# Pooled attention and two expert layers on one core: second layer's weights converted in pairs of blocks with their last addition on GpSimd, and the leading tiles' attention work put into other steps

## The chip, the cores and the metric

The kernel runs on one core of a Trainium2 chip. The metric is device time in microseconds (us), from the first to the last instruction of the program. Three executions of the kernel before took 1326.18, 1326.63 and 1329.12 us; their median, 1326.63 us, is its time.

## The reference

Everything is float32. With 12288 queries of 128 channels (`q`, multiplied by 8 after it is drawn), a map `kv` of 384 x 32 positions, and `d_ff = 2048`:

```
kv_pool = mean of kv over 4 x 4 windows            # 96 * 8 = 768 keys
k = v = kv_pool @ w_sr                             # 768 x 128
a = exp(s - max(s)),  s = q @ k.T / sqrt(128)
x = (a / (sum(a) + 1e-9)) @ v
h = x @ w_in;   g = h * sigmoid(1.702 * h);        x = g @ w_out     # layer 1
h = x @ w_in2;  g = h * clip(h + 3, 0, 6) / 6;     out = g @ w_out2  # layer 2
```

## The kernel before

**Two-part numbers.** A product of float32 numbers is made of three products of float32r numbers on TensorE. Each operand is split into a high part (`..h`, or `hi`, rounded by ScalarE, helper `act_hi`) and the rest (`..l`, or `lo`, mostly a subtraction on VectorE, `dve_lo`; for `q` on GpSimd, `pool_lo`). So one float32 product is low*high, high*high and high*low.

**The weights' conversion.** The four weight matrices reach the chip as float64 bit patterns, two 32-bit words for each weight, in 16 blocks of 512 columns (`ws`, 128 x 512 x 2 words; eight blocks for each layer). VectorE makes float32 of the words. `w_bits` has four instructions (L180, L183, L186, L190), `w_hi` one on ScalarE, and `w_lo` four on VectorE (L202, L205, a subtraction on L133, the last addition on L212). `w_lo` also asks for a later block's load. Blocks 0 to 4 are converted in the opening (`W_EARLY`, and the piece `W` of `FIRST`), blocks 5 to 15 in the steps of `W_STEPS`: `w_bits` at step s, `w_hi` and `w_lo` at s+1.

**The opening.** Loads of `kv` (12 of 512 KB) and of the first blocks stand in SP's queue; pooling and the product with `w_sr` are one chain of matmuls (L541), which yields `k` and `v`. Then the list `FIRST` gives the order in which TensorE makes scores of tiles 0 to 3 (`S`), transpositions (`T`) and products with `v` (`A`). A tile is 512 queries, 24 tiles in all.

**The steps.** The rest is a loop over 384 units (layer, tile, j), one unit a step: tiles 0 to 3 in layer 1 (steps 0 to 31), the same in layer 2 (steps 32 to 63), then two tiles after another, 16 steps for each layer. In step s TensorE does the first product of unit s (`unit_mm`, 6 matmuls into one of two PSUM buffers `h`) and the second product of unit s-3 (`unit_out`, 6 matmuls into `acc`). In between ScalarE applies GELU and splits off `gh`, VectorE makes `gl` (L133); in layer 2 ScalarE makes `r` (L446) and VectorE `g` (L450). The two PSUM buffers of `acc` are also those of the attention's products with `v`.

**Attention beside the steps.** Tables of step numbers put the attention of later tiles into the steps. Tiles 2 and 3 are transposed on TensorE (`T_STEPS_0`, L288, into the single PSUM buffer `st`, emptied by ScalarE to `eTh` and VectorE to `eTl`). From tile 4 on VectorE transposes 32 x 32 blocks (`V_STEPS`, L307), 16 DMAs move them (`D_STEPS`), and three steps split the result (`H_STEPS`: `eTh` on ScalarE, `eTl` on VectorE). The product with `v` follows in two halves (`AV_STEPS`, `av_mm`, L341). Scores (`S_STEPS`, L241) also use `st`; VectorE takes the maximum (L248) and ScalarE the exponential. GpSimd multiplies by the reciprocal sums (L280) and makes the low part of `q` (L136). The tables with `_0` hold for the first 64 steps. Within a step `ORDER` sets the order on ScalarE and VectorE.

The engines run their instructions in the order in which the program lists them (the scheduler is off).

Of the kernel before, what the change touches and what calls it, by code (L numbers as in the profile page):

```python
# [76 lines left out]
def tile_pooled_attention__moe_gelu__moe_hardswish(  # L77
# [39 lines left out]
    wi = {}  # L117
    wo = {}
    for m in (1, 2):
        wi[m] = [const.tile([P, DFF], F32R, name=f"wi{m}_{s}") for s in "hl"]  # L120
        wo[m] = [const.tile([P, DFF], F32R, name=f"wo{m}_{s}") for s in "hl"]
# [40 lines left out]
    w_todo = []  # L162
    w_ready = []
    w_half = []
    w_places = list(W_PLACES)

    def w_load(tag):
        w, src, cs = w_todo.pop(0)
        s = work.tile([P, WL, 2], U32, tag=tag, name="ws", bufs={"g": 3, "r": 2, "ws": 1}[tag])
        nc.sync.dma_start(out=s, in_=src[:, cs, :])  # L170
        w_ready.append((w, s, cs))

    def w_bits():


        w, ws, cs = w_ready.pop(0)
        upper = ws[:, :, 1]
        a = work.tile([P, WL], U32, tag="o", name="wa")
        b = work.tile([P, WL], U32, tag="wb", name="wb")
        nc.vector.tensor_scalar(  # L180
            out=a, in0=upper, scalar1=0x7FFFFFFF, scalar2=None, op0=ALU.bitwise_and
        )
        nc.vector.tensor_scalar(  # L183
            out=f(a), in0=f(a), scalar1=UPPER_MIN, scalar2=UPPER_MAX, op0=ALU.max, op1=ALU.min
        )
        nc.vector.tensor_scalar(  # L186
            out=b, in0=a, scalar1=3, scalar2=0x3FFFFFFF,
            op0=ALU.logical_shift_left, op1=ALU.bitwise_and,
        )
        nc.vector.scalar_tensor_tensor(  # L190
            out=a, in0=upper, scalar=0xC0000000, in1=b, op0=ALU.bitwise_and, op1=ALU.bitwise_or
        )
        w_half.append((w, ws, cs, a, b))
# [229 lines left out]
    for s in W_STEPS:  # L423
        at(s, "w_bits", w_bits)
        at(s + 1, "w_hi", w_hi)
        at(s + 1, "w_lo", w_lo)
# [63 lines left out]
    with tc.manual_schedule():  # L490
        make_identity(nc, ident)
        for m, src_i, src_o in ((1, w_in1, w_out1), (2, w_in2, w_out2)):
            blocks = [slice(o, o + WL) for o in range(0, DFF, WL)]
# [35 lines left out]
        for g_ in range(n_g):  # L529
            pk = big(*slots[g_])[:, 0, :kg]  # L530
            for w_ in range(n_w):
# [3 lines left out]
                if i in W_EARLY:  # L535
                    w_bits()
                    w_hi()
                    if i != W_EARLY[-1]:
                        w_lo()
# [114 lines left out]
```

## Time and profile before

| | |
|---|---|
| median of three executions | 1326.63 us (1326.18 to 1329.12) |
| span of the profiled execution | 1327.1 us |
| TensorE (PE) busy | 1299.5 us, 98% |
| VectorE (DVE) busy | 1038.1 us, 78% |
| ScalarE (ACT) busy | 1011.3 us, 76% |
| GpSimd (POOL) busy | 156.9 us, 12% |
| mean granted TensorE clock | 0.996 of full speed |

The profiled execution's span is the only time the page gives of it; no further time lies around it, and it is 0.5 us over the median of the three. Busy shares are averages over stages with different limits. A matmul is pipelined, so its busy time runs on while the next has begun; what counts on TensorE are the gaps, in which nothing ran, and the clock that was granted.

### The profile page before, as it was taken

How to read it: one execution, taken by the hardware profiler on the slowest of the kernel's cores; microseconds unless marked ns; L12 is line 12 of the kernel's file. 1: busy time of each engine (PE TensorE's matmuls, PEld its weight loads, DVE VectorE, ACT ScalarE, POOL GpSimd, SP SyncE). 2: the span in 40 equal slices, each digit the busy share in tenths (PEclk: the TensorE clock that was granted, in tenths of full speed). 3: DMA queues.
4: the chain of work that ended last, by engine and by line, in shares of the span. 5: the costliest groups of instructions: out<-in, count | busy, mean ns of one | idle time of the engine just before them, and what ended most of it. 6: DMA issues, size and time to landing. Idle time of an engine off the chain costs nothing.

```text
span 1327.1 us, 16044 instructions
## 1 busy us (share of the span) xinstructions
PE 1299.5 (98%) x5814; PEld 1077.7 (81%) x5814; DVE 1038.1 (78%) x1069; ACT 1011.3 (76%) x1191; POOL 156.9 (12%) x126
## 2 busy tenths in 40 slices
PE   8989999899999999999999999999999999999998
PEld 6778888777888888888888888788788888878887
DVE  6888899877688688688688688778768868858567
ACT  2777777668778778778878877787877877877876
POOL 0410003111011011011011002001101101100000
PEclk9999999999999999999999999999999999999999
DMA  8111102202202202201300400310220220210000
GB/s 319 41 48 48 33 16 64 64 8 61 51 16 57 56 16 56 56 17 30 82 9 11 108 9 9 86 26 17 62 50 17 56 56 9 56 48 8 9 1 17
DMA packets 26528, 59.84 MB, mean 45 GB/s; under 512 B 6352, under 2 KB 6480, under 8 KB 26448
## 3 DMA queue, kind: packets, MB, share of 16 engines
q1 hardware_dynamic: 26304, 58.75, 15.7%
q8 instruction: 46, 0.75, 0.2%
q14 instruction: 34, 0.28, 0.1%
q10 hardware_dynamic: 144, 0.07, 0.0%
HBM read 21.04 MB, written 6.29 MB: 21 GB/s over the span
## 4 chain that ended last, share of the span: by engine, by line
PE 84%; DVE 7%; ACT 3%; SPq 2%; issue 2%; DMA 2%; DVEq 0%; ACTq 0%
PE acc L473 12%; PE acc L474 12%; PE acc L475 12%; PE h L438 11%; PE h L437 11%; PE h L436 11%; PE acc L341 7%; PE st L241 6%; DVE gl L133 2%; SPq L317 2%; DVE eTl L133 1%; DMA kvs<-kvT 1%; DVE nm L248 1%; DMA q_f<-qT 1%; DVE g L450 1%
## 5 line engine op out<-in xcount | busy, mean ns | idle before, releaser
L133 DVE TENSOR_TENSOR gl<-g,gh 128x1024 fp32r<-128x1024 f32 x384 | 475.8, 1242 | 166.5 <-ACT gh L130 166.4
L130 ACT ACTIVATE gh<-g 128x1024 fp32r<-128x1024 f32 x384 | 405.3, 1058 | 23.7 <-PE acc L474 20.4
L446 ACT ACTIVATE r<-h 128x1024 f32<-128x1024 f32 x192 | 196.9, 1026 | 144.5 <-PE h L438 144.5
L473 PE MATMUL acc<-gh,wo_l 128*128 128x512 f32 x768 | 300.0, 391 | 0.5
L450 DVE SCALAR_TENSOR_TENSOR g<-r,h 128x1024 f32<-128x1024 f32 x192 | 234.1, 1219 | 84.0 <-ACT r L446 82.2
L475 PE MATMUL acc<-gl,wo_h 128*128 128x512 f32 x768 | 299.3, 390 | 0.4 <-DVE gl L133 0.4
L474 PE MATMUL acc<-gh,wo_h 128*128 128x512 f32 x768 | 299.3, 390 | 0.0
L442 ACT ACTIVATE g<-h 128x1024 f32<-128x1024 f32 x192 | 196.2, 1022 | 56.2 <-PE h L438 56.0
L473 PEld LDWEIGHTS acc<-gh,wo_l 128*128 128x128 f32 x768 | 144.3, 188 | 34.7 <-DVE x1l L133 4.3
L475 PEld LDWEIGHTS acc<-gl,wo_h 128*128 128x128 f32 x768 | 144.2, 188 | 31.1 <-DVE gl L133 0.8
L474 PEld LDWEIGHTS acc<-gh,wo_h 128*128 128x128 f32 x768 | 144.3, 188 | 30.7
L280 POOL TENSOR_SCALAR e<-e,rec 128x768 f32<-128x768 f32 x96 | 120.0, 1269 | 280.3 <-issue 201.5
L436 PE MATMUL h<-x1h,wi_l 128*128 128x512 f32 x384 | 150.8, 393 | 0.0
L438 PE MATMUL h<-x1l,wi_h 128*128 128x512 f32 x384 | 150.0, 391 | 0.0
L437 PE MATMUL h<-x1h,wi_h 128*128 128x512 f32 x384 | 149.9, 390 | 0.0
L436 PE MATMUL h<-x2h,wi_l 128*128 128x512 f32 x368 | 143.2, 389 | 1.2 <-DVE g L450 1.2
L438 PE MATMUL h<-x2l,wi_h 128*128 128x512 f32 x368 | 144.3, 392 | 0.0
L437 PE MATMUL h<-x2h,wi_h 128*128 128x512 f32 x368 | 144.0, 391 | 0.0
L136 POOL TENSOR_TENSOR q_l<-q_f,q_h 128x512 fp32r<-128x512 f32 x24 | 36.3, 1511 | 705.6 <-ACT q_h L130 705.6
L263 ACT ACTIVATE e<-st,nm 128x768 f32<-128x768 f32 x86 | 77.1, 896 | 13.1 <-DVE nm L248 13.0
L438 PEld LDWEIGHTS h<-x1l,wi_h 128*128 128x128 f32 x384 | 72.4, 188 | 15.3
L436 PEld LDWEIGHTS h<-x1h,wi_l 128*128 128x128 f32 x384 | 72.4, 188 | 15.0
(90 smaller groups left out, 1423.2 us busy)
## 6 DMA issues: line engine op xcount, KB each, us to landing
eTl<-e SPq DMA_DIRECT2D x320, 96.0 KB, 2.1
kvs<-kvT SPq DMA_DIRECT2D x12, 512.0 KB, 9.6
q_f<-qT SPq DMA_DIRECT2D x24, 256.0 KB, 2.6
outT<-o SPq DMA_DIRECT2D x24, 256.0 KB, 2.0
ws<-w_in SPq DMA_DIRECT2D x8, 512.0 KB, 4.6
ws<-w_out SPq DMA_DIRECT2D x8, 512.0 KB, 4.0
wsr_sb<-w_sr ACTq DMA_DIRECT2D x1, 64.0 KB, 4.7
```

Source lines behind the costliest of these rows:

```text
L130: nc.scalar.activation(hi, x, AF.Copy)
L133: nc.vector.tensor_tensor(out=lo, in0=x, in1=f(hi), op=ALU.subtract)
L280: nc.gpsimd.tensor_scalar(out=e, in0=e, scalar1=rec[:, r:r + 1], scalar2=1.0, op0=ALU.mult, op1=ALU.mult)
L436: nc.tensor.matmul(hp[:, c, :], wi[m][1][:, ch], xh, start=True, stop=False)
L437: nc.tensor.matmul(hp[:, c, :], wi[m][0][:, ch], xh, start=False, stop=False)
L438: nc.tensor.matmul(hp[:, c, :], wi[m][0][:, ch], xl, start=False, stop=True)
L442: nc.scalar.activation(g, h_t.pop(u), AF.Gelu_apprx_sigmoid)
L446: nc.scalar.activation(r, h_t[u], AF.Relu, bias=3.0)
L450: nc.vector.scalar_tensor_tensor(out=g, in0=r_t.pop(u), scalar=6.0, in1=h_t.pop(u), op0=ALU.min, op1=ALU.mult)
L473: nc.tensor.matmul(acc, wo[m][1][:, ch], gh[:, c, :], start=first, stop=False)
L474: nc.tensor.matmul(acc, wo[m][0][:, ch], gh[:, c, :], start=False, stop=False)
L475: nc.tensor.matmul(acc, wo[m][0][:, ch], gl[:, c, :], start=False, stop=last)
```

## The change

The conversion is cut into five parts: `a` and `b` (the four instructions of `w_bits`), `h` (the high part on ScalarE), `c` and `d` (the four of `w_lo`). The eight blocks of layer 1 are converted one at a time as before, those of layer 2 two at a time: each instruction then has 128 x 1024 elements. In these pairs the last addition goes to GpSimd. Raw words and the tiles `g` and `r` share one tile `slots` of five places; all high and low weights lie in `w_hl`; `w_a` and `w_b` have one buffer each, and the output tile `o` takes that of `w_a`. Block 5's parts `a`, `b`, `c` come at the end of `FIRST`, and the loads of blocks 5 to 7 are asked for one conversion later than before (block 5's stood between the last two pieces of `kv`). The step tables of tiles 2 to 5 change.

```diff
-T_STEPS_0 = {2: (4, 6, 8, 10), 3: (14, 16, 18, 20)}
-V_STEPS_0 = {4: (40, 41, 42, 43), 5: (48, 49, 50, 51)}
-D_STEPS_0 = {4: 44, 5: 52}
-H_STEPS_0 = {4: (47, 48, 49), 5: (55, 56, 57)}
-AV_STEPS_0 = {1: (1, 2), 2: (11, 12), 3: (21, 22), 4: (50, 51), 5: (58, 59)}
+T_STEPS_0 = {2: (7, 9, 11, 13), 3: (15, 17, 19, 21)}
+V_STEPS_0 = {4: (40, 41, 42, 43), 5: (50, 51, 52, 53)}
+D_STEPS_0 = {4: 44, 5: 54}
+H_STEPS_0 = {4: (48, 49, 50), 5: (58, 59, 60)}
+AV_STEPS_0 = {1: (1, 2), 2: (14, 14), 3: (22, 22), 4: (52, 53), 5: (61, 62)}
...
-    "S00 Q1 S01 S10 S02 S03 S11 T00 T01 T02 Q2 v T03 S12 S13 S20 A0 W Q3 T10 T11 T12 T13 S21 S22 "
-    "S23 S30 S31 S32 S33"
+    "S00 Q1 S01 S10 S02 S03 S11 T00 T01 T02 Q2 v T03 S12 S13 S20 A0 Wcd Q3 T10 T11 T12 T13 S21 S22 "
+    "S23 S30 S31 S32 S33 Wabc"
...
-W_LOADS = {0: "g", 2: "g", 4: "g", 6: "r", 8: "r", 10: "ws"}
-W_EARLY = (1, 3, 5, 7, 9)
-W_PLACES = "- - - r r ws r r ws r r - r r - -".split()
-W_STEPS = (0, 2, 5, 9, 12, 15, 18, 21, 24, 27, 29)
+W_LOADS = 0, 2, 4, 6, 8
+W_EARLY = {1: "abhcd", 3: "abhcd", 5: "abhcd", 7: "abhcd", 9: "abh"}
+W_SLOTS = 0, 1, 2, 3, 4, 3, 4, 3, 3
+W_NEXT = 0, 0, 0, 1, 1, 1, 0, 1, 1, 1, 1, 0
+W_STEPS = (
+    (0, "hdab"), (2, "hcd"), (3, "ab"), (5, "hcd"),
+    (8, "a"), (10, "b"), (12, "hc"), (14, "d"), (16, "a"), (18, "b"), (20, "hc"), (21, "d"),
+    (22, "a"), (23, "b"), (25, "hc"), (26, "d"), (27, "a"), (28, "b"), (30, "hc"), (31, "d"),
+)
...
+    w_hl = [const.tile([P, len(w_blocks), WL], F32R, name=f"w_{s}") for s in "hl"]
+    slots = const.tile([P, 5, 2 * TT], F32, name="slots")
...
+    def w_group(n):
+        k = len(w_blocks) // 2
+        if n < k:
+            return range(n, n + 1), W_SLOTS[n]
+        return range(2 * n - k, 2 * n - k + 2), W_SLOTS[-1]
...
+        if kind == "d":
+            dve_lo(w_a, w_a, hi)
+            add = nc.vector if k == 1 else nc.gpsimd
+            add.tensor_tensor(out=lo, in0=w_a, in1=w_b, op=ALU.add)
...
-        g_t[u] = g = work.tile([P, 2, TT], F32, tag="g", name="g", bufs=3)
+        g_t[u] = g = slot(u % 3)
...
-        r_t[u] = r = work.tile([P, 2, TT], F32, tag="r", name="r")
+        r_t[u] = r = slot(3 + u % 2)
...
-            o = work.tile([P, TT], F32, tag="o", name="o")
+            o = work.tile([P, TT], F32, tag="w_a", name="o", bufs=1)
```

What moves in the program is told below by rows of the instruction order, where a number at the end tells how often the row follows itself. First VectorE's rows from the last maximum of the opening on, in the kernel before (`wa`, `wb` are the conversion's tiles, `gl` is that of units 0 and 1):

```order
L248 TENSOR_REDUCE nm<-st 128x1
L276 TENSOR_SCALAR rec<-sums 128x4
L277 RECIPROCAL rec<-rec 128x4
L133 TENSOR_TENSOR gl<-g,gh 128x1024
L180 TENSOR_SCALAR wa<-ws 128x512
L183 TENSOR_SCALAR wa<-wa 128x512
L186 TENSOR_SCALAR wb<-wa 128x512
L190 SCALAR_TENSOR_TENSOR wa<-ws,wb 128x512
L133 TENSOR_TENSOR gl<-g,gh 128x1024
L202 TENSOR_SCALAR wb<-wa 128x512
```

And VectorE's rows from the same maximum on in the changed kernel:

```order
L283 TENSOR_REDUCE nm<-st 128x1
L218 TENSOR_SCALAR w_a<-slots 128x512
L221 TENSOR_SCALAR w_a<-w_a 128x512
L225 TENSOR_SCALAR w_b<-w_a 128x512
L229 SCALAR_TENSOR_TENSOR w_a<-slots,w_b 128x512
L236 TENSOR_SCALAR w_b<-w_a 128x512
L239 SCALAR_TENSOR_TENSOR w_b<-slots,w_b 128x512
L311 TENSOR_SCALAR rec<-sums 128x4
L312 RECIPROCAL rec<-rec 128x4
L152 TENSOR_TENSOR gl<-slots,gh 128x1024
L152 TENSOR_TENSOR w_a<-w_a,w_h 128x512
L247 TENSOR_TENSOR w_l<-w_a,w_b 128x512
```

Six of block 5's eight instructions now stand ahead of tile 3's reciprocals and of the first `gl`; its last two, and then block 6's first four, stand between the first and the second `gl`.

GpSimd's rows around the end of layer 1 in the kernel before (`q_l` is the low part of a tile's queries, `e` are the exponentials of a tile):

```order
L136 TENSOR_TENSOR q_l<-q_f,q_h 128x512
L280 TENSOR_SCALAR e<-e,rec 128x768 x8
L136 TENSOR_TENSOR q_l<-q_f,q_h 128x512 x2
L280 TENSOR_SCALAR e<-e,rec 128x24x32 x4
L136 TENSOR_TENSOR q_l<-q_f,q_h 128x512
```

And GpSimd's rows there in the changed kernel:

```order
L155 TENSOR_TENSOR q_l<-q_f,q_h 128x512
L315 TENSOR_SCALAR e<-e,rec 128x768 x8
L247 TENSOR_TENSOR w_l<-w_a,w_b 128x1024 x3
L155 TENSOR_TENSOR q_l<-q_f,q_h 128x512
L247 TENSOR_TENSOR w_l<-w_a,w_b 128x1024
L155 TENSOR_TENSOR q_l<-q_f,q_h 128x512
L315 TENSOR_SCALAR e<-e,rec 128x24x32 x4
```

Four additions of 128 x 1024 have come in, three of them ahead of tile 4's `q_l` and one behind it.

TensorE's rows from the end of step 50's second product on, in the kernel before (`acc<-eT` is tile 4's product with `v`, `st<-k` are scores):

```order
L475 MATMUL acc<-gl,wo_h 128x512
L341 MATMUL acc<-eTh,v_l 128x512 x3
L341 MATMUL acc<-eTh,v_h 128x512 x3
L341 MATMUL acc<-eTl,v_h 128x512 x3
L241 MATMUL st<-k_h,q_h 128x384 x2
L241 MATMUL st<-k_l,q_h 128x384 x2
L241 MATMUL st<-k_h,q_l 128x384 x2
```

TensorE's rows from the same place on in the changed kernel:

```order
L507 MATMUL acc<-gl,w_h 128x512
L276 MATMUL st<-k_h,q_h 128x384 x2
L276 MATMUL st<-k_l,q_h 128x384 x2
L276 MATMUL st<-k_h,q_l 128x384 x2
L468 MATMUL h<-x_1265,w_l 128x512
L469 MATMUL h<-x_1265,w_h 128x512
```

The product with `v` has left step 50; the scores follow the second product at once, and the next step's first product follows them. The nine matmuls stand two steps later.

## Rows read from the trace of the kernel before

**Rows 1.** From the page: TensorE's busy time, and the chain by engine.

```profile
PE 1299.5 (98%) x5814; PEld 1077.7 (81%) x5814; DVE 1038.1 (78%) x1069; ACT 1011.3 (76%) x1191; POOL 156.9 (12%) x126
PE 84%; DVE 7%; ACT 3%; SPq 2%; issue 2%; DMA 2%; DVEq 0%; ACTq 0%
```

**Rows 2.** Stretches: length, each engine's busy time (instructions), granted clock, DMA share, GB/s.

```profile
26.00:28.00 2.00, 1.96 (x10) 1.41 (x9) 1.90 (x7) 0.38 (x1) 0.00 (x0) 1.00 1.04 412
60.00:90.00 30.00, 25.88 (x115) 21.20 (x114) 24.06 (x37) 22.96 (x29) 8.38 (x8) 0.94 0.12 36
90.00:180.00 90.00, 88.14 (x406) 72.58 (x405) 78.92 (x109) 68.78 (x79) 1.41 (x1) 1.00 0.13 39
500.00:600.00 100.00, 99.86 (x448) 83.08 (x447) 77.09 (x75) 79.97 (x94) 13.26 (x10) 1.00 0.16 43
221.04:293.88 72.84, 67.10 (x289) 55.40 (x289) 61.77 (x60) 48.22 (x62) 14.14 (x10) 0.95 0.19 49
```

**Rows 3.** Timeline of TensorE: start, length, instruction, idle before it and what ended that.

```profile
83.46 1.15 PE L288 MATMUL st<-ident,e 128*128 128x128 f32 x6 [4.00 <-DVE eTl L133]
104.37 0.50 PE L341 MATMUL acc<-eTh,v_l 128*128 128x512 f32 x1 [0.68 <-DVE x2l L133]
177.81 0.50 PE L436 MATMUL h<-x2h,wi_l 128*128 128x512 f32 x1 [1.18 <-DVE g L450]
236.37 0.97 PE L341 MATMUL acc<-eTh,v_l 128*128 128x512 f32 x3 [3.14 <-ACT eTh L130]
271.17 1.31 PE L341 MATMUL acc<-eTh,v_l 128*128 128x512 f32 x3 [2.33 <-ACT eTh L130]
322.53 0.73 PE L341 MATMUL acc<-eTh,v_l 128*128 128x512 f32 x2 [1.29 <-ACT eTh L130]
```

**Rows 4.** Timeline of VectorE at the end of the opening and in step 0.

```profile
62.50 0.96 DVE L248 TENSOR_REDUCE nm<-st 128x1 f32<-128x768 f32 x1 [0.38 <-PE st L241]
64.59 0.44 DVE L276 TENSOR_SCALAR rec<-sums 128x4 f32<-128x4 f32 x1 [1.13 <-ACT e L263]
67.95 1.23 DVE L133 TENSOR_TENSOR gl<-g,gh 128x1024 fp32r<-128x1024 f32 x1 [2.71 <-ACT gh L130]
69.55 0.94 DVE L183 TENSOR_SCALAR wa<-wa 128x512 f32<-128x512 f32 x1
71.59 1.22 DVE L133 TENSOR_TENSOR gl<-g,gh 128x1024 fp32r<-128x1024 f32 x1
```

**Rows 5.** Groups of instructions by form: count, busy time, mean ns of one, idle before.

```profile
L133 DVE TENSOR_TENSOR gl<-g,gh 128x1024 fp32r<-128x1024 f32 x384 | 475.8, 1242 | 166.5 <-ACT gh L130 166.4
L133 DVE TENSOR_TENSOR eTl<-st,eTh 128x768 fp32r<-128x768 f32 x10 | 9.5, 950 | 0.1
L183 DVE TENSOR_SCALAR wa<-wa 128x512 f32<-128x512 f32 x16 | 7.4, 460 | 0.5
L212 DVE TENSOR_TENSOR wi_l<-wa,wb 128x512 fp32r<-128x512 f32 x8 | 5.5, 692 | 0.3
L307 DVE STREAM_TRANSPOSE e<-e 128x768 f32<-128x768 f32 x80 | 76.4, 963 | 0.0
L136 POOL TENSOR_TENSOR q_l<-q_f,q_h 128x512 fp32r<-128x512 f32 x24 | 36.3, 1511 | 705.6 <-ACT q_h L130 705.6
```

**Rows 6.** Timeline of GpSimd and VectorE where the two run at once.

```profile
166.92 1.41 POOL L136 TENSOR_TENSOR q_l<-q_f,q_h 128x512 fp32r<-128x512 f32 x1 [96.71 <-ACT q_h L130]
167.08 2.33 DVE L133 TENSOR_TENSOR gl<-g,gh 128x1024 fp32r<-128x1024 f32 x1
226.74 2.78 POOL L280 TENSOR_SCALAR e<-e,rec 128x768 f32<-128x768 f32 x2 [4.95 <-DVE rec L277]
226.87 1.87 DVE L133 TENSOR_TENSOR eTl<-eTl,eTh 128x1024 fp32r<-128x1024 f32 x1 [0.23 <-issue]
```

**Rows 7.** Timeline of TensorE's weight loads at the last `kv` piece.

```profile
27.55 0.19 PEld L541 LDWEIGHTS st<-kvs,wsr_sb 128*128 128x128 f32 x1 [0.44 <-DMA kvs<-kvT]
```

More of the change, by code (lines that the diff above doesn't have):

```diff
@@ L116, in tile_pooled_attention__moe_gelu__moe_hardswish, with chunk, slot @@
     v_l = const.tile([P, KC, C], F32R, name="v_l")
[L117 to L121, printed above, removed]
+    w_blocks, w_at = [], {}
+    for m, src_i, src_o in ((1, w_in1, w_out1), (2, w_in2, w_out2)):
+        blocks = range(DFF // WL)
+        for side, k in sorted(
+            [("i", k) for k in blocks] + [("o", k) for k in blocks],
+            key=lambda x: (max(x[1] * 2 + 3 * (x[0] == "o"), 0), x[0]),
+        ):
+            w_at[side, m, k] = len(w_blocks)
+            w_blocks.append((src_i if side == "i" else src_o, slice(k * WL, (k + 1) * WL)))
+    w_hl = [const.tile([P, len(w_blocks), WL], F32R, name=f"w_{s}") for s in "hl"]
+    slots = const.tile([P, 5, 2 * TT], F32, name="slots")
+    def chunk(side, m, n):
+        k, c = divmod(n, WL // P)
+        return (x[:, w_at[side, m, k], c * P:(c + 1) * P] for x in w_hl)
+    def slot(n):
+        return slots[:, n].rearrange("p (c k) -> p c k", k=TT)
     def f(ap):
@@ L159, in split_q @@
         load_q(t + 1)
[L162 to L193, printed above, removed]
@@ L349, in split_acc @@
     def split_acc(acc, tag, place=None):
-        if place == "ws":
-            both = work.tile([P, 2, TT], F32R, tag="ws", name=tag, bufs=1)
-            hi, lo = both[:, 0, :], both[:, 1, :]
-        else:
-            hi, lo = (
-                work.tile([P, TT], F32R, tag=place or tag + s, name=tag + s) for s in "hl"
-            )
+        if place is not None:
+            both = work.tile([P, 2, TT], F32R, tag=place, name=tag, bufs=1)
+            hi, lo = both[:, 0], both[:, 1]
+        else:
+            hi, lo = (work.tile([P, TT], F32R, tag=tag + s, name=tag + s) for s in "hl")
         act_hi(hi, acc)
@@ L422, in tile_pooled_attention__moe_gelu__moe_hardswish @@
             at(step, "table", exp_table)
[L423 to L426, printed above, removed]
+    for step, kinds in W_STEPS:
+        for kind in kinds:
+            at(step, "w_hi" if kind == "h" else "w", w_step, kind)
     h_t, r_t, g_t, gs_t, acc_t = {}, {}, {}, {}, {}
@@ L535, in tile_pooled_attention__moe_gelu__moe_hardswish @@
                 if i in W_EARLY:
[L536 to L539, printed above, removed]
+                    for kind in W_EARLY[i]:
+                        w_step(kind)
                 for w in range(kw // kg):
@@ L575, in piece @@
             elif kind == "W":
-                w_lo()
+                for step in name[1:]:
+                    w_step(step)
             else:
```

117 lines of the change are left out of this document (74 added, 43 removed).

## The prediction

> **What bounds the kernel now.** I read the page first: TensorE is busy in 98% of the span and has 84% of the chain [rows 1], so only a TensorE gap or a slow clock can be won. The table of stretches, next, shows where there is one: from 500 to 600 us TensorE stands still for 0.14 of 100 us, from 60 to 90 us for 4.1 of 30 at a mean clock of 0.94, and from 221 to 294 us for 5.7 of 72.8 at 0.95 [rows 2]. The order of instructions from step 64 on is the same in both kernels, so the change can only act ahead of that, some 294 us into the span. The timeline of TensorE names each gap there and what ended it [rows 3]: 4.00 us at 83 us (a transposition of tile 2 waits for `st`, which VectorE empties late), 0.68 at 104 (PSUM `acc` held by VectorE's `x2l`), 1.18 at 178 (`h` held by VectorE's `g`), and 3.14 and 2.33 at 236 and 271 us, where the product with `v` waits for `eTh`. All come from a VectorE that is late. In the opening TensorE runs through scores and pooling with small waits of which the change touches one [rows 7].
>
> **The opening.** Block 5's load no longer stands between the last two pieces of `kv`. The DMA engines are full there (share 1.04, 412 GB/s [rows 2]), so 512 KB less ahead of the last piece lets it land 512 KB / 412 GB/s = 1.3 us earlier; TensorE waited 0.44 us for it [rows 7], and no more can be won. I take 0.4, from 0 to 0.4.
>
> **Block 5's six instructions, steps 0 to 9.** By [rows 5] one block costs VectorE four single-input instructions of 0.46 us and four two-input ones of 0.69: 4.6 us. Parts `a`, `b` and `c` are four of 0.46 and two of 0.69, 3.2 us. They go where VectorE is idle: between the last maximum and the first `gl` it stands still for 1.13 + 2.71 = 3.8 us [rows 4]. Tile 2's two early transpositions leave steps 4 and 6 too, with 2 x 0.95 us of VectorE [rows 5], so by step 6 VectorE has 5.1 us less to do than before, more than the 4.00 us that TensorE waited. That wait goes, and with it the slow clock that followed: 0.06 x 30 = 1.8 us [rows 2]. Full gain 5.8.
>
> It isn't free, though. Tile 3's reciprocals now stand behind the six, so GpSimd's four scalings for tile 3 start some 2.5 us later and run beside step 0. What that does is seen in [rows 6]: a subtraction of `eTl` that began with a scaling took 1.87 us in place of 1.2, and two scalings took 2.78 us with the subtraction in between; a `gl` behind a `q_l` took 2.33 us. The two engines take turns, an instruction at a time, when VectorE reads two tensors of SBUF; in [rows 4] the single-input L183 took 0.94 in place of 0.43. A scaling alone is (2.78 - 1.2) / 2 = 0.8 us; four can hold VectorE for up to 3.2 us, I take 2.3, and block 5's last two instructions (1.3 us) now stand ahead of the second `gl`. It would end at 71.59 + 1.22 + 1.3 + 2.3 = 76.4 us. TensorE, without the transposition in step 4, asks for it at about 75.0: a new wait of 1.4. I put another 1.0 at the second transposition, where VectorE is still late by that. Taken: 5.8 - 2.4 = 3.4. Ends: 5.8 without holds; 1.2 if the new waits grow to 2.9 and cost a slow clock of 1.7 again.
>
> **Products of tile 2, and the end of layer 1.** At step 14 the product with `v` finds `acc` free (tile 0's `x2l` is four steps back): 0.7 us won. At 178 us VectorE came late to `g` because a `gl` had been held 1.1 us by `q_l` [rows 6] and the last block's eight instructions ran in steps 29 and 30. Now there is one part a step and ScalarE's `h` part finds its input two steps old: 1.2 us won, or 0.
>
> **Pairs, and the addition on GpSimd, steps 8 to 31.** A pair has four single-input instructions of twice the columns; bounds 0.46 (nothing added) and 0.92 (doubled), taken in the middle, 0.69. Its two-input ones are bounded by 0.69 and 1.38; a `gl` of the same shape takes 1.24 [rows 5], which I take. Seven stay on VectorE: 4 x 0.69 + 3 x 1.24 = 6.5 us in place of 9.2, so 11 us less on VectorE for four pairs. None of it shows by itself: from 90 to 180 us TensorE is busy 88.1 of 90 us and VectorE idle for 11 [rows 2]. The four additions on GpSimd are wider than any in the trace; from `q_l` of half the columns, 1.5 to 3.0 us each [rows 5], taken 2.8 (twice the undisturbed 1.41). Behind each waits the next `gl` if it is ready sooner, and behind that the units' second product, three steps later; that distance hides it, and the 11 us in which VectorE is idle, with the 11 us freed. The next pair's part `a` waits for the addition too (one buffer of `w_a`), but stands behind that same `gl`. Taken 0; if one hold of 2.5 us reaches TensorE, -2.5. GpSimd is idle from about 70 to 167 us [rows 6], so no queue forms there.
>
> The Trainium skill, "GPSIMD Engine Reference", section 3, speaks against this edit: a two-input addition takes GpSimd about twice as long as VectorE, so elementwise work stays on VectorE. By its ratio of 1.96 the addition would take 1.24 x 1.96 = 2.4 us, an estimate by that page; the sum would not change, since neither engine is the bound in those steps. The same page's section 8 says that VectorE's instructions with two SBUF inputs contend with GpSimd; the trace agrees (1.87 us in place of 1.2).
>
> **Tiles 4 and 5, steps 47 to 62.** Two gaps, 3.14 + 2.33 = 5.5 us, and slow clock of 0.05 x 72.84 = 3.6 us [rows 2, 3]: 9.1 in all. Tile 4's product now comes two steps after its last `eTh`, not one; a step is at least 2.7 us of TensorE. Tile 5's block transpositions, 0.96 us each [rows 5], two of them ahead of that `eTh`, now come after it: 2.7 + 1.9 = 4.6 us more room against a wait of 3.14. For tile 5 the distance stays one step, but three steps without `eTl` lie ahead, and GpSimd's scalings, which held two of VectorE's instructions in that place, are past. But VectorE was busy for 61.8 us of this stretch [rows 2], which would shrink to 72.8 - 9.1 = 63.7 us: 97% busy, and tile 4's DMAs and `st` tie it to the others at every step. So I leave 1.1 us of it unwon and take 8.0; ends 9.1 and 4. At step 67 `acc` is freed later than before, by the last output of tile 3 (the buffers' turns have changed); up to 1 us, but it lies ahead of the 1.29 us at 322 us, whose `eTh` doesn't wait for it [rows 3], so it costs nothing on top.
>
> **Sum.** 0.4 + 3.4 + 0.7 + 1.2 + 0 + 8.0 = 13.7 us. From the profiled span of 1327.1 that is 1313.4; the median lies 0.5 lower, so 1313.0 us, rounded. Best ends: 0.4 + 5.8 + 0.7 + 1.2 + 9.1 = 17.2, 1309.4 us. Worst ends: 1.2 + 0.7 + 4 - 2.5 = 3.4, 1323.2.
>
> **Rivals.**
> - A. VectorE is the bound of steps 47 to 63. With the product's 4 us of matmuls taken out of steps 50 and 51, TensorE reaches the next `h` sooner than VectorE makes `g`, and small waits replace the two large ones. For it: 97% busy. Against: the large waits also cost 3.6 us of clock, which small ones need not. It would win 2 of the 8.0 us: 13.7 - 6 = 7.7, 1319 us.
> - B. The opening's six instructions come too late: if GpSimd's scalings hold them as they hold L183, the first `gl` slips past 70 us and the gap at 83 us returns a step earlier with its clock, longer by the 2 us of block 6's first four instructions that now stand ahead of the second `gl`; and steps 50 to 62 are as in A. Then 0.7 + 1.2 + 2 - 2 = 2, 1325 us. Against: 3.8 us of idle time is there to be read.
> - C. Slower: GpSimd's additions hold VectorE at each pair, in steps 14, 21, 26 and 31, and it decides when VectorE is already a step late there, as it was at 167 us: then each hold, 2.8 us, reaches TensorE, and each makes the clock fall for 1.7 us, as after the gaps of 2.33 us and more. 4 x 4.5 = 18 us against 13.7: 1331 us. For it: that `gl` of 2.33 us stood ahead of the 1.18 us gap. Against: VectorE has 11 + 11 us of room in these steps. By the skill's section 3 above this is the expected side; the trace's idle time says no.
> - D. The new step tables do not do what they say: the two waits for `eTh` return in full at the later steps, and only the opening and layer 1 win, 13.7 - 8.0 = 5.7 us, 1321 us. For it: for tile 5 the distance is as short as before. Its chance is counted with A's.
>
> **How the numbers follow.** My forecast has 0.68, A (with D) 0.18, B 0.08, C 0.06. The range: the forecast's own ends are 1309.4 and 1323.2; most of A lies inside; 1309 to 1322 leaves out 2 in 10. A difference under 0.2%, 2.7 us, can't be told from none in a measurement of this kernel. Faster by more: forecast, A and a little of B, 0.88. Same: most of B, 0.06. Slower: C, 0.06.
>
> **What would show it.** Right: no TensorE gap over 2 us between 60 and 290 us, and a granted clock of 1.00 from 221 us to step 64; VectorE's six instructions ahead of the first `gl`, which begins by 69 us; step 64 about 13 us sooner than at 293.9 us; the same distance from there to the end. Wrong: gaps at `h` in steps 50 to 62 (A), a gap of `gl` in step 4 over 3 us (B), `gl` of over 3 us in steps 14 to 32 with TensorE waiting (C), or a span from step 64 on that differs by over 2 us, which I have no term for.

## The result, and the profile after

The changed kernel takes 1315.06 us (median of four executions, 1314.66 to 1316.82), the kernel before 1327.51 (median of four, the three of the section on the time before among them): a ratio of 0.9903, 95% interval 0.9891 to 0.9914, so 12.5 us faster. The profiled execution has a span of 1313.4 us and took 1315.17; 1.8 us lie around the span.

The page of the kernel after, as in [rows 1]: TensorE's busy time and the chain. VectorE's share is what it was.

```profile
PE 1294.4 (99%) x5814; PEld 1074.4 (82%) x5814; DVE 1029.6 (78%) x1033; ACT 1010.7 (77%) x1187; POOL 167.5 (13%) x130
PE 84%; DVE 7%; ACT 3%; issue 2%; SPq 2%; DMA 1%; POOL 0%; ACTq 0%; DVEq 0%; POOLq 0%
```

Stretches of the kernel after (columns as in [rows 2]): the first two are those of [rows 2], the third is steps 50 to 63.

```profile
60.00:90.00 30.00, 27.89 (x130) 22.42 (x128) 28.99 (x41) 25.54 (x32) 9.66 (x8) 1.00 0.15 50
90.00:180.00 90.00, 89.40 (x414) 74.09 (x413) 72.66 (x74) 69.34 (x76) 13.08 (x5) 1.00 0.12 40
224.93:280.36 55.43, 54.59 (x248) 45.59 (x247) 50.65 (x51) 40.83 (x53) 7.81 (x7) 1.00 0.16 44
```

The granted clock is 1.00 in all of them (0.94 from 60 to 90 us and 0.95 from 221 to 294 us in [rows 2]). TensorE's timeline after, the waits that answer to [rows 3] and one new one:

```profile
75.36 0.50 PE L507 MATMUL acc<-gl,w_h 128*128 128x512 f32 x1 [0.77 <-DVE gl L152]
89.37 0.85 PE L323 MATMUL st<-ident,e 128*128 128x128 f32 x6 [1.22 <-DVE eTl L152]
172.38 0.50 PE L468 MATMUL h<-x2h,w_l 128*128 128x512 f32 x1 [0.60 <-DVE slots L482]
258.80 0.62 PE L276 MATMUL st<-k_h,q_h 128*128 128x384 f32 x2 [0.72 <-ACT e L298]
308.62 0.98 PE L376 MATMUL acc<-eTh,v_l 128*128 128x512 f32 x3 [0.91 <-ACT eTh L149]
```

The gap of 4.00 us at a transposition is 1.22, tile 2's product waits no more, the wait of `h` at the end of layer 1 is 0.60 in place of 1.18, and the two waits for `eTh` of 3.14 and 2.33 us are gone; the scores of tile 7 (258.80) wait 0.72 us in their place. All of TensorE's gaps over 0.15 us, without the first one of 5.5 us that ends with the load of `w_sr`, are 8.6 us, in before 17.1; between the start of step 0 and that of step 64 they are 3.3 and 11.6.

For every kernel below the profile was read at the first matmul of steps 0, 17, 34, 50, 64 and 74. Lengths in us, of one profiled execution each (a slow clock in that execution is part of them):

| kernel | median | steps 0–16 | 17–33 | 34–49 | 50–63 | 64–73 |
|---|---|---|---|---|---|---|
| before | 1327.4 (15 runs) | 61.39 | 54.20 | 52.52 | 63.54 | 30.90 |
| after | 1315.06 | 56.96 | 53.75 | 52.55 | 55.43 | 30.52 |
| old tables of tiles 4, 5 | 1321.19 | 56.94 | 53.74 | 52.55 | 64.01 | 30.37 |
| before, new tables of 4, 5 | 1320.99 | 62.55 | 54.19 | 52.55 | 55.55 | 30.34 |
| last addition on VectorE | 1315.59 | 56.96 | 53.92 | 52.50 | 55.41 | 30.06 |
| no pairs | 1317.30 | 57.69 | 54.38 | 52.51 | 55.54 | 30.56 |
| block 5 in the steps | 1316.76 | 58.43 | 53.74 | 52.52 | 55.47 | 30.48 |
| old tables of tiles 2, 3 | 1319.82 | 62.06 | 53.61 | 52.50 | 55.45 | 30.19 |
| before, load later | 1326.99 | 61.41 | 54.20 | 52.53 | 60.93 | 30.49 |
| spread | 1316.42 | 58.50 | 52.99 | 52.37 | 55.40 | 30.21 |
| pairs earlier | 1313.18 | 55.80 | 52.99 | 52.37 | 55.40 | 30.17 |
| block 6 later | 1312.43 | 55.06 | 52.99 | 52.37 | 55.42 | 30.07 |

From step 64 to the end both kernels take the same (1033.2 us before, 1033.0 after).

### The profile page after: what moved, and what is told of

It is laid out like the page before. It is cut to its first block, busy times and chain, and to the rows that moved or that the text cites. A ratio compares the mean times of both kernels' runs of the same rounds, so it can differ in the third digit from the quotient of the medians.

```text
span 1313.4 us, 16024 instructions
## 1 busy us (share of the span) xinstructions
PE 1294.4 (99%) x5814; PEld 1074.4 (82%) x5814; DVE 1029.6 (78%) x1033; ACT 1010.7 (77%) x1187; POOL 167.5 (13%) x130
## 4 chain that ended last, share of the span: by engine, by line
PE 84%; DVE 7%; ACT 3%; issue 2%; SPq 2%; DMA 1%; POOL 0%; ACTq 0%; DVEq 0%; POOLq 0%
PE acc L505 12%; PE acc L506 12%; PE acc L507 12%; PE h L470 11%; PE h L469 11%; PE h L468 11%; PE acc L376 7%; PE st L276 6%; SPq L352 2%; DVE gl L152 1%; DVE eTl L152 1%; ACT eTh L149 1%; DMA eTl<-e 1%; DVE nm L283 1%; DVE x1l L152 1%
## 5 line engine op out<-in xcount | busy, mean ns | idle before, releaser
L152 DVE TENSOR_TENSOR gl<-slots,gh 128x1024 fp32r<-128x1024 f32 x384 | 474.2, 1238 | 164.6 <-ACT gh L149 164.4
L149 ACT ACTIVATE gh<-slots 128x1024 fp32r<-128x1024 f32 x384 | 405.3, 1058 | 24.4 <-PE acc L506 20.2
L478 ACT ACTIVATE slots<-h 128x1024 f32<-128x1024 f32 x192 | 197.0, 1026 | 135.9 <-PE h L470 135.8
L507 PE MATMUL acc<-gl,w_h 128*128 128x512 f32 x768 | 299.4, 390 | 1.2 <-DVE gl L152 1.2
L505 PE MATMUL acc<-gh,w_l 128*128 128x512 f32 x768 | 299.9, 391 | 0.5
L506 PE MATMUL acc<-gh,w_h 128*128 128x512 f32 x768 | 299.3, 390 | 0.0
L482 DVE SCALAR_TENSOR_TENSOR slots<-slots,h 128x1024 f32<-128x1024 f32 x192 | 234.0, 1219 | 79.0 <-ACT slots L478 77.0
L474 ACT ACTIVATE slots<-h 128x1024 f32<-128x1024 f32 x192 | 196.1, 1021 | 50.5 <-PE h L470 50.4
L468 PE MATMUL h<-x1h,w_l 128*128 128x512 f32 x384 | 150.3, 391 | 0.0
L470 PE MATMUL h<-x1l,w_h 128*128 128x512 f32 x384 | 149.5, 389 | 0.0
L469 PE MATMUL h<-x1h,w_h 128*128 128x512 f32 x384 | 149.5, 389 | 0.0
L298 ACT ACTIVATE e<-st,nm 128x768 f32<-128x768 f32 x86 | 77.0, 895 | 13.3 <-DVE nm L283 11.6
```

What stands on the lines that cost most here:

```text
L149: nc.scalar.activation(hi, x, AF.Copy)
L152: nc.vector.tensor_tensor(out=lo, in0=x, in1=f(hi), op=ALU.subtract)
L468: nc.tensor.matmul(hp[:, c, :], wl, xh, start=True, stop=False)
L469: nc.tensor.matmul(hp[:, c, :], wh, xh, start=False, stop=False)
L470: nc.tensor.matmul(hp[:, c, :], wh, xl, start=False, stop=True)
L482: nc.vector.scalar_tensor_tensor(out=g, in0=r_t.pop(u), scalar=6.0, in1=h_t.pop(u), op0=ALU.min, op1=ALU.mult)
```

## The experiments

**Tiles 4 and 5: the new step numbers taken out of the changed kernel, and put alone into the kernel before.**

```diff
-V_STEPS_0 = {4: (40, 41, 42, 43), 5: (50, 51, 52, 53)}
-D_STEPS_0 = {4: 44, 5: 54}
-H_STEPS_0 = {4: (48, 49, 50), 5: (58, 59, 60)}
-AV_STEPS_0 = {1: (1, 2), 2: (14, 14), 3: (22, 22), 4: (52, 53), 5: (61, 62)}
+V_STEPS_0 = {4: (40, 41, 42, 43), 5: (48, 49, 50, 51)}
+D_STEPS_0 = {4: 44, 5: 52}
+H_STEPS_0 = {4: (47, 48, 49), 5: (55, 56, 57)}
+AV_STEPS_0 = {1: (1, 2), 2: (14, 14), 3: (22, 22), 4: (50, 51), 5: (58, 59)}
```

> The changed kernel with the old step numbers for tiles 4 and 5 (block transpositions, DMAs, splits and products), all else new. Theory: the stretch of steps 50 to 63 won its 8.1 us by these numbers alone, so the two waits of the product with v for eTh come back, about 3.1 and 2.3 us long, with a stretch at half the granted clock behind each; start of step 50 to start of step 64 takes 63.5 us in place of 55.4 and the time is 1315.1 + 8.1 = 1323 us (1321 to 1324). Rival: the shared tile of g and r, or VectorE's lighter layer 1, brought it; then 1315 us and no gap over 1 us there.

> The kernel before with only the new step numbers for tiles 4 and 5. Theory: 1327.5 - 8.1 = 1319.4 us (1318 to 1321), with the gaps at 83 and 178 us unchanged and none over 1 us from step 50 to 63. Rival (it takes the relief of VectorE in layer 1 as well, or the new buffers): 1327 us, or a part of the gain only, 1323 us.

Measured: 1321.19 us (ratio to before 0.9958 [0.9946, 0.9971]) and 1320.99 (0.9949 [0.9937, 0.9962]). The changed kernel with the old numbers, TensorE's timeline, and the stretch from each of the two waits on:

```profile
231.17 1.22 PE L376 MATMUL acc<-eTh,v_l 128*128 128x512 f32 x2 [3.14 <-ACT eTh L149]
266.46 0.73 PE L376 MATMUL acc<-eTh,v_l 128*128 128x512 f32 x2 [2.02 <-ACT eTh L149]
```

```profile
231.10:235.00 3.90, 3.83 (x9) 3.09 (x10) 3.90 (x5) 2.36 (x4) 0.00 (x0) 0.50 0.18 68
266.40:270.40 4.00, 3.94 (x13) 3.28 (x14) 3.71 (x4) 2.36 (x4) 0.00 (x0) 0.69 0.17 66
```

Both waits are back, with a granted clock of 0.50 (1.2 GHz) for 3.9 us behind the first and a mean of 0.69 behind the second. Put alone into the kernel before, the numbers shorten steps 50 to 63 by 8.0 us and nothing else. (Steps 0 to 16, whose instructions are the same, were 1.2 us longer in that execution, at a mean clock of 0.95 against 0.97: differences of that size there can be the clock's.) So the tables do it alone; the lighter layer 1 and the shared tile have no part in it. Which of the four tables does it, and how much is tile 4's and how much tile 5's, was not taken apart. The medians moved less than expected, 6.1 and 6.4 us, because the clock does not fall each time. The five executions with the old numbers have the same program and take 1320.8, 1320.9 and 1321.2 us at a mean clock of 1.000, and 1323.5 and 1323.9 at 0.996: some 2.7 us that come and go. The profiled one was one of the latter.

**The pairs' last addition on VectorE; and no pairs at all.**

```diff
-            add = nc.vector if k == 1 else nc.gpsimd
-            add.tensor_tensor(out=lo, in0=w_a, in1=w_b, op=ALU.add)
+            nc.vector.tensor_tensor(out=lo, in0=w_a, in1=w_b, op=ALU.add)
```

> The changed kernel with the pairs' last addition on VectorE. Theory: neither engine bounds steps 8 to 31, so the time stays at 1315 us within 0.7; the 2.3 us for which part a waits for GpSimd's addition at 159 us goes, and the TensorE gap of 0.60 us at 172 us with it, which would make 1314.5 us. Rival 1: the additions had to leave VectorE: four of 1.2 us come back and reach TensorE, 1317 to 1320 us. Rival 2: the holds by GpSimd had cost more than the one gap: 1313 us.

```diff
-W_SLOTS = 0, 1, 2, 3, 4, 3, 4, 3, 3
-W_NEXT = 0, 0, 0, 1, 1, 1, 0, 1, 1, 1, 1, 0
+W_SLOTS = 0, 1, 2, 3, 4, 3, 4, 3, 4, 3, 4, 3, 4, 3, 4, 3
+W_NEXT = 0, 0, 0, 1, 1, 1, 1, 1, 1, 1, 1, 1, 1, 1, 0, 0
...
-    (8, "a"), (10, "b"), (12, "hc"), (14, "d"), (16, "a"), (18, "b"), (20, "hc"), (21, "d"),
-    (22, "a"), (23, "b"), (25, "hc"), (26, "d"), (27, "a"), (28, "b"), (30, "hc"), (31, "d"),
+    (9, "ab"), (10, "hcd"), (12, "ab"), (13, "hcd"), (15, "ab"), (16, "hcd"), (18, "ab"), (19, "hcd"),
+    (21, "ab"), (22, "hcd"), (24, "ab"), (25, "hcd"), (27, "ab"), (28, "hcd"), (29, "ab"), (30, "hcd"),
...
-        if n < k:
-            return range(n, n + 1), W_SLOTS[n]
-        return range(2 * n - k, 2 * n - k + 2), W_SLOTS[-1]
+        return range(n, n + 1), W_SLOTS[n]
```

> The changed kernel with layer 2's blocks converted one at a time on VectorE, at the steps of the kernel before (9 and 10 to 29 and 30). Theory: the pairs bring nothing, 1315 us within 1; step 17 begins at the same 118.6 us; the wait of h for g at the change of layers is 0.6 to 1.2 us. Rival: the pairs, with the 11 us that they take off VectorE, carry what steps 8 to 34 won (some 1 us), and with the next blocks' work VectorE is late again in steps 8 to 14: 1317 to 1319 us with gaps at tile 2's transpositions.

Measured: 1315.59 us (0.991 [0.9896, 0.9923]) and 1317.30 (0.9921 [0.9907, 0.9934]). GpSimd's additions, its timeline in the kernel after:

```profile
114.64 2.40 POOL L247 TENSOR_TENSOR w_l<-w_a,w_b 128x1024 fp32r<-128x1024 f32 x1 [41.01 <-DVE w_a L152]
155.92 3.32 POOL L247 TENSOR_TENSOR w_l<-w_a,w_b 128x1024 fp32r<-128x1024 f32 x1 [14.79 <-DMA slots<-w_out]
161.32 1.65 POOL L155 TENSOR_TENSOR q_l<-q_f,q_h 128x512 fp32r<-128x512 f32 x1 [2.09 <-ACT q_h L149]
```

and what VectorE did meanwhile:

```profile
155.75 1.22 DVE L152 TENSOR_TENSOR gl<-slots,gh 128x1024 fp32r<-128x1024 f32 x1
159.26 0.69 DVE L218 TENSOR_SCALAR w_a<-slots 128x1024 uint32<-128x1024 uint32 x1 [2.29 <-POOL w_l L247]
159.99 0.69 DVE L221 TENSOR_SCALAR w_a<-w_a 128x1024 f32<-128x1024 f32 x1
160.60 1.22 DVE L152 TENSOR_TENSOR gl<-slots,gh 128x1024 fp32r<-128x1024 f32 x1
161.74 1.79 DVE L225 TENSOR_SCALAR w_b<-w_a 128x1024 uint32<-128x1024 uint32 x1
```

The addition at 155.92 waited for the `gl` that began 0.17 us ahead of it and then took 2.3 us; VectorE lost 2.29 us to it, because the next pair's part `a` needs the buffer, and with the addition on VectorE it pays 1.23 us for each instead. The two come out alike: steps 17 to 33 differ by 0.17 us, the medians by 0.5, within their spread. My expectation that the 0.60 us at 172 us would go is wrong; with the addition on VectorE they became 0.77:

```profile
173.40 0.50 PE L467 MATMUL h<-x2h,w_l 128*128 128x512 f32 x1 [0.77 <-DVE slots L481]
```

Without pairs TensorE has one wait more, at a transposition of tile 2 as the rival said, and the wait at the change of layers is 1.19 us in place of 0.60:

```profile
102.62 0.63 PE L320 MATMUL st<-ident,e 128*128 128x128 f32 x4 [0.60 <-DVE eTl L152]
...
173.96 0.50 PE L465 MATMUL h<-x2h,w_l 128*128 128x512 f32 x1 [1.19 <-DVE slots L479]
```

Steps 0 to 33 are 1.4 us longer. The profiled span is 2.1 us longer; of the rest, 0.2 us lie ahead of step 0 and some 0.5 from step 64 on, at waits for `eTh` (941 us, 0.98 in place of 0.46 us), where the two kernels have the same order of instructions; that one wait is between 0.37 and 1.22 us in the profiles here. So the pairs, with the steps that they stand in, bring some 1.4 us; where the addition runs brings nothing that these runs can tell.

**Steps 0 to 16: block 5 back in the steps; and the old numbers of tiles 2 and 3.**

```diff
-    "S23 S30 S31 S32 S33 Wabc"
+    "S23 S30 S31 S32 S33"
...
-    (0, "hdab"), (2, "hcd"), (3, "ab"), (5, "hcd"),
+    (0, "ab"), (1, "hcd"), (2, "ab"), (3, "hcd"), (5, "ab"), (6, "hcd"),
```

> The changed kernel without the piece Wabc: blocks 5, 6 and 7 are converted at the steps of the kernel before (0 and 1, 2 and 3, 5 and 6). Theory: the new numbers of tile 2's transpositions carry the gain of steps 0 to 9, and the early parts only move work ahead of the first gl that GpSimd then holds; without them the wait of 0.77 us at gl goes and the one at the second transposition grows from 1.2 to about 2.5 us: 1315 to 1317 us. Rival (the prediction's own sum, in which the six instructions are 3.2 of 5.1 us of relief): the gap of about 4 us is back with its slow clock, 1318 to 1320 us.

```diff
-T_STEPS_0 = {2: (7, 9, 11, 13), 3: (15, 17, 19, 21)}
-AV_STEPS_0 = {1: (1, 2), 2: (14, 14), 3: (22, 22), 4: (52, 53), 5: (61, 62)}
+T_STEPS_0 = {2: (4, 6, 8, 10), 3: (14, 16, 18, 20)}
+AV_STEPS_0 = {1: (1, 2), 2: (11, 12), 3: (21, 22), 4: (52, 53), 5: (61, 62)}
```

> The changed kernel with the old numbers for tiles 2 and 3 (transpositions from steps 4 and 14, products at 11, 12 and 21, 22). Theory: VectorE reaches the first transposition's low part only at about 82.5 us, after the conversions that stand ahead of it; the second one, in step 6, waits some 4 us, the clock falls behind it, and the 0.7 us at tile 2's product is back: 1319 to 1321 us. Rival (block 5's early parts carry the gain): a gap of at most 1.2 us, 1315 to 1316 us.

Measured: 1316.76 us (0.9917 [0.9904, 0.9931]) and 1319.82 (0.9941 [0.9928, 0.9953]). With block 5 in the steps TensorE waits here:

```profile
80.70 0.50 PE L468 MATMUL h<-x1h,w_l 128*128 128x512 f32 x1 [1.49 <-ACT slots L474]
...
91.54 0.63 PE L323 MATMUL st<-ident,e 128*128 128x128 f32 x4 [1.67 <-DVE eTl L152]
```

and with the old numbers of tiles 2 and 3 here, the stretch behind it at half the clock:

```profile
83.59 0.66 PE L323 MATMUL st<-ident,e 128*128 128x128 f32 x2 [4.27 <-DVE eTl L152]
```

```profile
83.50:87.50 4.00, 3.91 (x13) 3.36 (x14) 3.93 (x6) 0.81 (x1) 0.00 (x0) 0.50 0.02 4
```

The numbers of tiles 2 and 3 together are worth 62.06 − 56.96 = 5.1 us of steps 0 to 16, block 5's early parts 58.43 − 56.96 = 1.5 (in the version without them blocks 6 and 7 are converted one or two steps later too). The version with the old numbers has the early parts and all else that is new, and still its steps 0 to 16 take 62.06 us, inside the 61.39 to 62.55 that they take in the three profiles without the early parts and with the old numbers, and the gap is 4.27 us against 4.00: it wins nothing there. The early parts alone were not put into the kernel before. One thing that I expected of the old numbers did not come: the wait at tile 2's product is 0.13 us and not 0.7.

**The load of block 5, alone in the kernel before.**

```diff
-W_LOADS = {0: "g", 2: "g", 4: "g", 6: "r", 8: "r", 10: "ws"}
-W_PLACES = "- - - r r ws r r ws r r - r r - -".split()
+W_LOADS = {0: "g", 2: "g", 4: "g", 6: "r", 8: "r"}
+W_PLACES = "- - - ws r r ws r r ws r r r r - -".split()
```

> The kernel before with block 5's load asked for one conversion later (and each later load too), so that it no longer stands between the last two pieces of kv; nothing else. Theory: the opening's term alone; the wait of 0.44 us at the last piece goes and step 0 begins 0.4 to 0.6 us sooner; the rest is as before, 1327 us. Rival: the start of step 0 does not move, and the 0.56 us between the two kernels there come from the conversion of the blocks in the opening.

Measured: 1326.99 us, a ratio of 1.0000 [0.9991, 1.0008]. Step 0 begins at 61.89 us, in before at 62.23. But over all profiled executions it begins between 61.67 and 62.53 us with the load moved (nine kernels and the kernel after), and at 61.96 in the other one without. The wait itself is gone: with the load moved none of the ten profiles has idle time of the weight loads at the last piece, and the two without have 0.44 and 0.16 us. But a term of 0.4 us at step 0 can't be told from the spread of its start; what it is worth in time stays open.

**Three waits that are left.** One version moves all three causes:

```diff
-    (0, "hdab"), (2, "hcd"), (3, "ab"), (5, "hcd"),
-    (8, "a"), (10, "b"), (12, "hc"), (14, "d"), (16, "a"), (18, "b"), (20, "hc"), (21, "d"),
-    (22, "a"), (23, "b"), (25, "hc"), (26, "d"), (27, "a"), (28, "b"), (30, "hc"), (31, "d"),
+    (0, "hd"), (1, "ab"), (2, "hcd"), (3, "ab"), (5, "hcd"),
+    (8, "a"), (10, "b"), (11, "hc"), (12, "d"), (14, "a"), (15, "b"), (16, "hc"), (17, "d"),
+    (19, "a"), (20, "b"), (22, "hc"), (23, "d"), (25, "a"), (26, "b"), (28, "hc"), (29, "d"),
-T_STEPS_0 = {2: (7, 9, 11, 13), 3: (15, 17, 19, 21)}
+T_STEPS_0 = {2: (6, 9, 11, 13), 3: (15, 17, 19, 21)}
```

> The changed kernel with other steps for the conversion and for one transposition, to take away three gaps that are left: block 6's first four instructions go behind the second gl (0.77 us at 75 us), tile 2's first transposition goes from step 7 to 6 (1.2 us at 89 us), and pairs 2 to 4 go two steps earlier, so that VectorE has steps 30 and 31 to catch up (0.60 us at 172 us). Theory (each gap is VectorE late by the work that stands ahead in its queue): all three go, 2.6 us, 1312.5 us, a span of 1310.8. Rival: the sum of VectorE's work in steps 0 to 8 is what is late, whatever its order; the first two gaps move a step or two on and only the third goes, 1314.5 us.

The new numbers move more than is said there: the last parts of pair 1 go one and two steps earlier, pair 2 two to four, pair 3 three and pair 4 two.

Measured: 1316.42 us (0.9912 [0.9897, 0.9927]), no faster than the changed kernel. The three waits are gone, but a fourth is there. Its timeline of ScalarE, of TensorE, and the stretch behind:

```profile
71.57 1.06 ACT L149 ACTIVATE gh<-slots 128x1024 fp32r<-128x1024 f32 x1
76.21 0.63 ACT L149 ACTIVATE w_h<-w_a 128x512 fp32r<-128x512 f32 x1 [3.59 <-DVE w_a L229]
76.75 0.58 ACT L149 ACTIVATE x1h<-acc 128x512 fp32r<-128x512 f32 x1
77.23 1.01 ACT L474 ACTIVATE slots<-h 128x1024 f32<-128x1024 f32 x1
```

```profile
78.30 0.50 PE L468 MATMUL h<-x1h,w_l 128*128 128x512 f32 x1 [2.06 <-ACT slots L474]
```

```profile
79.80:83.30 3.50, 3.50 (x12) 2.77 (x11) 3.40 (x6) 3.44 (x4) 0.00 (x0) 0.52 0.00 0
```

ScalarE stood 3.59 us at block 6's high part, whose input VectorE now made after the second `gl`; a GELU was queued behind it, and TensorE waited for that one's `h`, 2.06 us and a slow clock. So two versions more: the spread one without that move of block 6 ("pairs earlier"), and with the high part moved too ("block 6 later"; block 7's parts and pair 1's first part stand a step later as well). The diff is from the first to the second:

```diff
-    (0, "hdab"), (2, "hcd"), (3, "ab"), (5, "hcd"),
-    (8, "a"), (10, "b"), (11, "hc"), (12, "d"), (14, "a"), (15, "b"), (16, "hc"), (17, "d"),
+    (0, "hd"), (1, "ab"), (3, "hcd"), (4, "ab"), (6, "hcd"),
+    (9, "a"), (10, "b"), (11, "hc"), (12, "d"), (14, "a"), (15, "b"), (16, "hc"), (17, "d"),
```

> The changed kernel with pairs 2 to 4 two steps earlier and tile 2's first transposition in step 6, the first layer's blocks as in the changed kernel (the part of the spread version that found no new wait). Theory: the gaps of 1.22 us at 89 and of 0.60 at 172 us go, the 0.77 at 75 us stays: 1315.1 - 1.8 = 1313.3 us, a span of 1311.6. Rival: VectorE is late in steps 4 to 8 by the sum of its work; the transposition in step 6 moves the 1.2 us to another wait, 1314.5 us.

> As the version with the pairs earlier, and block 6's first four instructions in step 1, its high part on ScalarE a step later too (step 3), block 7 in steps 4 and 6. Theory: in the spread version ScalarE stood still 3.6 us for block 6's high part, whose input had been moved behind the second gl, and the GELU behind it made TensorE wait 2.1 us; with the high part moved as well ScalarE waits for nothing, the 0.77 us at 75 us go too, 1312.5 us. Rival: VectorE's lateness at the third gl alone holds the place of g that the GELU of step 5 writes, and the wait at h stays, over 1 us: 1314 us or more.

Measured: 1313.18 us (0.9892 [0.9874, 0.9909]) and 1312.43 (0.9886 [0.987, 0.9902]). The last one beats both kernels: its four executions (1312.10 to 1313.05) all lie under the fastest of the changed kernel. ScalarE still waits 1.08 us at the same instruction, where none was expected, but the 0.77 us at `gl` are gone and no wait at `h` has come, and TensorE runs from 60 to 90 us with 29.64 of 30 us busy:

```profile
75.67 0.63 ACT L149 ACTIVATE w_h<-w_a 128x512 fp32r<-128x512 f32 x1 [1.08 <-DVE w_a L229]
```

```profile
60.00:90.00 30.00, 29.64 (x138) 24.20 (x137) 29.00 (x41) 27.05 (x34) 10.45 (x8) 1.00 0.08 21
```

## Why the prediction was right, term by term

The span came out as the sum said, 1313.4 us; that it did so to a tenth is luck. By the two profiles the gain is 0.56 us ahead of step 0 (said 0.4), 4.43 in steps 0 to 16 (4.1), 0.45 in steps 17 to 33 (1.2), nothing in steps 34 to 49, 8.11 in steps 50 to 63 (8.0) and 0.2 from step 64 on (0): a miss of 0.75 us is made good by small ones the other way. The terms one by one:

- **The opening, 0.4 us:** 0.56 in the two profiles. That the wait at the last piece goes is shown, that step 0 moves by it is not.
- **Tiles 4 and 5, 8.0 us:** right, 8.1 in the profile, and shown by the tables alone. Of it some 5.5 us are lasting, the two waits; the rest is the clock, which falls in some executions only. In the kernel before with the load moved, which has the old numbers, the two waits are there at a clock of 1.00, and steps 50 to 63 take 60.93 us; they took 63.54 and 64.01 in two others with the old numbers. I had put the clock's part at 3.6 us and left 1.1 of the whole unwon; 63.54 − 60.93 makes it 2.6. Of rival A the waits of scores for `st` are a trace, 0.72 us; rival D fell.

```profile
236.04 0.50 PE L341 MATMUL acc<-eTh,v_l 128*128 128x512 f32 x1 [3.13 <-ACT eTh L130]
269.78 0.50 PE L341 MATMUL acc<-eTh,v_l 128*128 128x512 f32 x1 [2.29 <-ACT eTh L130]
```

```profile
230.03:290.96 60.93, 54.88 (x247) 45.40 (x246) 52.51 (x51) 39.81 (x52) 9.73 (x7) 1.00 0.15 40
```

- **Steps 0 to 16, 3.4 + 0.7 us:** 4.4 measured, right in size (by one profile each, in which the clock can be 1 us either way) and half wrong in cause. I wrote that VectorE has 5.1 us less to do by step 6, 3.2 of them by block 5's early parts. Those parts are worth 1.5 us, and with the old numbers all of the new conversion together wins nothing there: the later blocks moved up as well. Ahead of step 4's transposition, VectorE had 16 conversion instructions in the steps before, and has 14 now (two of block 5, eight of block 6, four of block 7), and GpSimd's scalings fall into them. What won is that the transpositions leave steps 4 and 6 (5.1 us by the old numbers). Of the 0.7 us at tile 2's product the wait is gone in the kernel after; that the product's step took it away is not shown, since with the old step it was 0.13 us, when TensorE came there later. The new waits were put at 1.4 us at `gl` and 1.0 at the second transposition; they are 0.77 and 1.22. Rival B fell.
- **GpSimd beside VectorE at the end of the opening:** right. VectorE's timeline after, answering to [rows 4]:

```profile
61.94 0.96 DVE L283 TENSOR_REDUCE nm<-st 128x1 f32<-128x768 f32 x1 [0.39 <-PE st L276]
62.81 1.00 DVE L218 TENSOR_SCALAR w_a<-slots 128x512 uint32<-128x512 uint32 x1
63.85 1.02 DVE L221 TENSOR_SCALAR w_a<-w_a 128x512 f32<-128x512 f32 x1
64.90 0.43 DVE L225 TENSOR_SCALAR w_b<-w_a 128x512 uint32<-128x512 uint32 x1
...
67.45 1.21 DVE L152 TENSOR_TENSOR gl<-slots,gh 128x1024 fp32r<-128x1024 f32 x1
...
69.30 1.20 DVE L247 TENSOR_TENSOR w_l<-w_a,w_b 128x512 fp32r<-128x512 f32 x1
...
70.87 0.94 DVE L221 TENSOR_SCALAR w_a<-w_a 128x512 f32<-128x512 f32 x1
71.85 1.02 DVE L225 TENSOR_SCALAR w_b<-w_a 128x512 uint32<-128x512 uint32 x1
72.90 1.27 DVE L229 SCALAR_TENSOR_TENSOR w_a<-slots,w_b 128x512 uint32<-128x512 uint32 x1
74.09 2.35 DVE L152 TENSOR_TENSOR gl<-slots,gh 128x1024 fp32r<-128x1024 f32 x2
```

  The six instructions stand where VectorE was idle, the first `gl` begins at 67.45 us (said: by 69), the second, first of the two from 74.09 on, ends at some 75.3 (said: 76.4). From 69.30 on the scalings hold four instructions for 0.5 to 0.6 us each, 2.2 us in all (said: 2.3); the first two of the six are held as well, by tile 2's scalings, which I had not counted.
- **End of layer 1, 1.2 us, and pairs, 0:** 0.45 us measured in steps 17 to 33, and it is the pairs' (without them these steps take 54.38 us, in before 54.20). The step that failed is that the new places of the last parts make `g` early: from 160 us on VectorE has no idle time until it has made the first `g` of layer 2. In the kernel after `a` waited 2.29 us for GpSimd and `L225` was held by `q_l` (1.79 us), but with the addition on VectorE, where that first wait is not there, the gap is 0.77 us; that points to the sum of VectorE's work ahead of that `g`, and not to the one wait. With the pairs earlier, the last by two steps, the whole 1.2 us came (52.99 against 54.20). The pairs' freed time, which I put at nothing, is worth some 1.4 us of steps 0 to 33. Rival C's hold is there at 155.92 (3.32 us, and 3.33 at 137.79), but TensorE lost 0.6 us by it at the most, and no clock.
- **Sizes of the unseen instructions** were near: pairs' two-input ones 1.22 us (1.24), single-input ones 0.69 (0.69), GpSimd's addition 2.40 alone and 3.3 behind a `gl` (2.8):

```profile
L239 DVE SCALAR_TENSOR_TENSOR w_b<-slots,w_b 128x1024 f32<-128x1024 uint32 x4 | 4.9, 1226 | 0.1
L221 DVE TENSOR_SCALAR w_a<-w_a 128x1024 f32<-128x1024 f32 x4 | 2.8, 695 | 0.1
```

  By the Trainium skill, "GPSIMD Engine Reference", section 3, it would take twice VectorE's time; the trace agrees, with 2.40 us against 1.23 for the same addition on VectorE (the version with the last addition there).
- **From span to median:** 2.1 us off. I took the profiled span of before for its whole time, as the section on the time before has it, and that is wrong: in every later run 1.7 to 1.9 us lie around the span, so that execution took some 1328.9 us (an estimate from its span of 1327.1), 1.5 above the median of 1327.4: its mean clock was 0.996, with a slow clock behind the waits at 83, 236 and 271 us. The 15 executions of before in the table range from 1325.9 us at a mean clock of 0.999 to 1329.7 at 0.995.

## What to carry to other kernels

Where one engine is at 98%, look for its few gaps and ask which queue was late by how much; here a step's number in a table was worth more (5.1 and 8 us) than the work saved (1.4 and 1.5 us). When a piece of work is moved, move its consumer on the other engine by as much: an engine that runs in the program's order, as here, passes on the wait of its first blocked instruction to all that stand behind it. And take a clock that fell in the profiled execution as a gain that only part of the executions will show.
